# Order of the four pooled-value products of a head pair: by rows first, by heads second

## The chip, the cores and the metric

The kernel runs on one NeuronCore of one Trainium2 chip. The metric is the device time of one execution in microseconds, the median of several runs. TensorE appears in the profile as two engines: PE (matmuls) and PEld (loads of the stationary operand). DVE is VectorE, ACT ScalarE, POOL GpSimd, SP the engine that issues the DMAs.

## The reference

Three layers follow each other. The first is attention over 4 x 8 heads, 576 positions and 64 channels a head, and it is a sum of two parts: a local one (a band of keys around each query) and a pooled one, which the change touches:

```python
q_d = q.reshape(B, H, Sd, factor, D).mean(axis=3)      # factor 4, Sd = 144
k_d = k.reshape(B, H, Sd, factor, D).mean(axis=3)
v_d = v.reshape(B, H, Sd, factor, D).mean(axis=3)
out_d = sm_attn(q_d, k_d, v_d)                         # softmax(q_d k_d^T) v_d
out_up = np.repeat(out_d, factor, axis=2)
...
return (out_up + out_local).astype(np.float32)
```

The second layer is a gated feed-forward (512 to 1024 channels, a convolution of three taps, a sigmoid gate, 1024 back to 512). The third mixes positions with a product of rank 32 and ends with a feed-forward of 512 to 2048 to 512 channels with a ReLU, added to its input.

## The kernel before

The 32 heads are worked on as 16 pairs; the two heads of a pair lie on the partitions 0 to 63 and 64 to 127. All work of all layers is issued in one order written out by hand, the string `SEQ`: each word is a function with its arguments, such as `V.6.0` for the local value products of pair 6 or `Vd.6` for its pooled ones. Each engine runs its part of that list strictly in the order of the list, and waits where data are missing. Attention pairs, the second layer's products (lines 834 and 888) and the decoding of weights are interleaved there up to about 235 us; the third layer follows.

For a pair the pooled part goes so: scores (line 525), their maximum (530), the exponential (537), the division (542), the transposition by TensorE (575 and 576), the copy of the transposed weights to `PTd` (595 to 598), and then `pv_pooled` (from line 611). The 144 pooled keys do not fit on 128 partitions, so they are split into 112 and 32. The values of the first 112 keys lie in `vd`. The last 32 keys of four pairs share one tile `ve`, each pair on its own 32 partitions (`rest(p)`), and `PTd` is split in the same manner. So each head needs two products that add up in PSUM: one that contracts over 112 rows, and one over 32 rows. Each product has 64 stationary columns (a head's channels) and 144 moving columns (the queries). Head 0 writes to the partitions 0 to 63 of the tile `O`, head 1 to 64 to 127, in the same PSUM bank. Data are float32, and the trace shows each product as two weight loads and two matmuls, so a pair's four products are eight of each.

Just before them in `SEQ`, as a rule, stands `pv_local` (line 608): 24 products with 64 rows and 64 stationary columns each. They use the two row halves and the two column halves of the array in turn. Behind the pooled products `copy_od` (`xd`, lines 625 and 627) and `add_x` (line 636) take the sum out of `O`. In the earlier pairs the words `f.n` add filler matmuls (`beat`, line 390) that write to a spare part of the tile used last; where that is `O`, its readers wait for them as well.

The buffers `vd`, `ve` and `PTd` are used again by later pairs, whose pooled sums of values (`vsum`, line 558) and copies wait for the last product that reads the buffer.

Of the kernel before, what the change touches and what calls it, by code (L numbers as in the profile page):

```python
# [276 lines left out]
def mixer_kernel(ctx, tc, consts, qk, vw_, vr_, vz_, w1, w2, cw_, u_, v_, out, outT):  # L277
    nc = tc.nc
# [5 lines left out]
    D = P // 2  # L284
# [9 lines left out]
    SD, NM = S // 4, 112  # L294
# [272 lines left out]
    def rest(p):  # L567
        return slice(32 * (p % 4), 32 * (p % 4) + 32)
# [42 lines left out]
    def pv_pooled(p):  # L611
        e = st[p]
        pt = e["PTd"].rearrange("p c (j r) -> p c j r", j=3)
        for h in range(2):
            o = e["O"][D * h:D * h + D, 0, 288:288 + SD].rearrange("p (j r) -> p j r", j=3)
            to, cols = slice(48 * h, 48 * h + 48), slice(D * h, D * h + D)
            nc.tensor.matmul(o, e["vd"][:, cols], pt[:NM, 0, :, to], start=True, stop=False)  # L617
            nc.tensor.matmul(o, e["ve"][rest(p), cols], pt[rest(p), 1, :, to], start=False, stop=True)  # L618

    def copy_od(p, eng):  # L620
        e = st[p]
# [585 lines left out]
    def flush_t(r, blk, c):  # L1207
# [10 lines left out]
        "Sd": scores_d, "Md": maxima_d, "Ed": exps_d, "nd": lambda p: norm_d(p, GP), "ndv": lambda p: norm_d(p, DV),  # L1218
        "vs": vsum, "vsv": lambda p, i: vsum(p, i, DV), "T": trans, "Td": trans_d, "c": lambda p: copy_T(p, "ACT"), "cv": lambda p: copy_T(p, "DVE"),
        "cd": lambda p: copy_Td(p, A), "cdv": lambda p: copy_Td(p, V), "V": pv_local, "Vd": pv_pooled,  # L1220
        "xd": lambda p: copy_od(p, "ACT"), "xdv": lambda p: copy_od(p, "DVE"), "x": add_x,
        "wl": w_load, "wd": lambda *k: w_dec(DV, *k), "wp": lambda *k: w_dec(GP, *k), "wh": w_hi, "wo": lambda *k: w_lo(GP, *k), "wO": lambda *k: w_lo(DV, *k),
# [96 lines left out]
```

## Time and profile before

| | |
|---|---|
| runs | 714.07, 714.94, 718.48 us; median 714.94 us |
| the profiled execution's own time | 717.92 us |
| its span, first to last instruction | 716.1 us |
| mean granted TensorE clock | 0.989 of 2.4 GHz |
| busy time of PE, PEld, DVE, ACT, POOL | 701.1, 636.6, 543.5, 433.2, 340.7 us |
| instructions in the span | 15851 |

The busy times come from one profiled execution, whose time is 3.0 us above the median of the runs. Busy time of PE counts a matmul from its issue to its modelled end, so neighbouring matmuls overlap and a drained array can still count as busy; idle time of the array at a change between products is seen better on PEld. A granted clock of 1.00 is 2.4 GHz, one of 0.50 is 1.2 GHz.

### The profile page before, as it was taken

The numbers are of one execution on the slowest core, as the hardware profiler recorded it, in microseconds if no ns is written. First come the engines' busy times: TensorE is split into PE (matmuls) and PEld (weight loads), VectorE is DVE, ScalarE is ACT, GpSimd is POOL, SyncE is SP. The second block draws the span as 40 slices with busy tenths as digits, with TensorE's granted clock in tenths as the row PEclk, the third lists the DMA queues.
The fourth block names the chain that finished last, engine by engine and source line by source line (L and its number), as shares of the span: only waits on it lengthen the run. The fifth ranks groups of instructions, "written<-read, shape, count | busy, mean of one in ns | idle before, by whom it ended". The sixth has DMA issues, their size and how long they took to land.

```text
span 716.1 us, 15851 instructions
## 1 busy us (share of the span) xinstructions
PE 701.1 (98%) x5937; PEld 636.6 (89%) x5937; DVE 543.5 (76%) x963; ACT 433.2 (60%) x1005; POOL 340.7 (48%) x353
## 2 busy tenths in 40 slices
PE   6999999999999999999999999999999999999997
PEld 4878788888888888898999988899999999999997
DVE  4878998878876877789886666577756797667777
ACT  4778888676576776888755555555434465443431
POOL 2246465135233553558465646134734463554543
PEclk9979999999999999999999999999999999999999
DMA  8777543534443340224889989889887768687765
GB/s 292 223 248 261 172 138 143 189 126 153 156 127 127 116 133 31 88 89 141 274 284 305 312 299 318 297 274 313 286 277 224 242 195 271 219 278 246 252 205 180
DMA packets 75388, 152.22 MB, mean 213 GB/s; under 512 B 8176, under 2 KB 16624, under 8 KB 75312
## 3 DMA queue, kind: packets, MB, share of 16 engines
q1 hardware_dynamic: 75312, 151.22, 63.2%
q8 instruction: 47, 0.77, 0.5%
q14 instruction: 29, 0.24, 0.1%
HBM read 111.34 MB, written 39.85 MB: 211 GB/s over the span
## 4 chain that ended last, share of the span: by engine, by line
PE 89%; DMA 3%; DVE 2%; issue 2%; POOL 2%; ACT 1%; SPq 1%; DVEq 0%; POOLq 0%; ACTq 0%
PE g L1045 24%; PE acc L888 14%; PE g L834 13%; PE acc L1077 9%; PE xa L1198 8%; PE ya L1198 4%; PE za L1198 2%; PE O L608 2%; PE O L617 1%; PE S L459 1%; PE Sd L525 1%; PE O L618 1%; DMA wb<-t 1%; PE h L912 1%; POOL w L721 1%
## 5 line engine op out<-in xcount | busy, mean ns | idle before, releaser
L1045 PE MATMUL g<-bt,as 128*128 128x384 f32 x1008 | 197.0, 338 | 0.5 <-DMA as<-s 0.5
L1045 PEld LDWEIGHTS g<-bt,as 128*128 128x128 f32 x1008 | 178.6, 188 | 5.3 <-issue 1.0
L834 PE MATMUL g<-xhl,w 128*128 128x386 f32 (+1 forms) x576 | 119.0, 346 | 0.8 <-DVE ghl L880 0.8
L888 PE MATMUL acc<-w,ghl 128*128 128x512 f32 x432 | 114.1, 397 | 0.4 <-DVE ghl L880 0.4
L834 PEld LDWEIGHTS g<-xhl,w 128*128 128x128 f32 x576 | 101.9, 190 | 6.8 <-issue 1.4
L1184 POOL TENSOR_TENSOR rt<-fr,rt 128x384 fp32r<-128x384 f32 x64 | 65.6, 1038 | 62.4 <-ACT rt L1180 56.0
L888 PEld LDWEIGHTS acc<-w,ghl 128*128 128x128 f32 x432 | 79.2, 188 | 15.0 <-issue 1.0
L1205 DVE TENSOR_TENSOR uT<-uT,xa 128x384 f32<-128x384 f32 x128 | 69.1, 551 | 30.0 <-PE xa L1198 29.3
L880 POOL TENSOR_TENSOR ghl<-ct,ghl 128x384 fp32r<-128x384 f32 x40 | 42.7, 1068 | 87.1 <-ACT ghl L877 72.8
L1198 PE MATMUL xa<-rt,wb 128*128 128x384 f32 x384 | 82.4, 337 | 0.1
L1184 POOL TENSOR_TENSOR rt<-tp,rt 128x384 fp32r<-128x384 f32 x48 | 50.5, 1063 | 53.0 <-ACT rt L1180 34.9
L1077 PE MATMUL acc<-w,a 128*128 128x512 f32 x288 | 73.7, 394 | 0.0
L1050 ACT ACTIVATE tp<-g 128x384 f32<-128x384 f32 x72 | 35.2, 488 | 63.5 <-PE g L1045 62.0
L861 DVE SCALAR_TENSOR_TENSOR g<-h,cw,g 128x384 f32<-128x384 f32 x96 | 59.3, 618 | 14.0 <-ACT g L856 12.7
L1198 PEld LDWEIGHTS xa<-rt,wb 128*128 128x128 f32 x384 | 67.8, 188 | 1.0 <-DVE uT L1205 0.8
L1054 DVE TENSOR_TENSOR tp<-g,tp 128x384 f32<-128x384 f32 x72 | 40.0, 555 | 33.5 <-PE g L1045 31.5
L1077 PEld LDWEIGHTS acc<-w,a 128*128 128x128 f32 x288 | 53.2, 188 | 8.7
L1180 ACT ACTIVATE rt<-fr 128x384 fp32r<-128x384 f32 x64 | 32.6, 520 | 25.6 <-PE za L1198 9.2
L1198 PE MATMUL ya<-rt,wb 128*128 128x384 f32 x192 | 42.5, 337 | 1.8 <-DMA wb<-t 1.8
L1205 DVE TENSOR_TENSOR uT<-uT,ya 128x384 f32<-128x384 f32 x64 | 34.6, 549 | 9.6 <-PE ya L1198 9.6
L1107 POOL TENSOR_TENSOR l<-s,l 128x256 fp32r<-128x256 f32 x28 | 22.7, 815 | 34.3 <-ACT l L1103 34.3
L721 POOL TENSOR_TENSOR w<-wval,w 128x512 fp32r<-128x512 f32 x17 | 22.8, 1348 | 28.7 <-ACT w L718 22.8
(182 smaller groups left out, 1303.7 us busy)
## 6 DMA issues: line engine op xcount, KB each, us to landing
as<-s SPq DMA_DIRECT2D x112, 256.0 KB, 4.2
wb<-t SPq DMA_DIRECT2D x112, 256.0 KB, 4.2
s<-as SPq DMA_DIRECT2D x56, 256.0 KB, 3.2
raw<-in_w_dram SPq DMA_DIRECT2D x26, 512.0 KB, 5.1
zraw<-in_w_dram SPq DMA_DIRECT2D x22, 512.0 KB, 4.3
qk<-in_qk_dram SPq DMA_DIRECT2D x16, 576.0 KB, 5.3
t<-l SPq DMA_DIRECT2D x28, 256.0 KB, 2.9
vw<-in_vw_dram SPq DMA_DIRECT2D x16, 384.0 KB, 4.3
```

Source lines behind the costliest of these rows:

```text
L834: nc.tensor.matmul(gp[n][:, :wd], w[:, a, cc], xhl[g, cc][:, b, :wd], start=cc == 0 and i == 0, stop=cc == NCC - 1 and i == 2)
L861: nc.vector.scalar_tensor_tensor(out=o, in0=inner(g, hts[n], k), scalar=cw[:, k * NF + f:k * NF + f + 1], in1=o, op0=ALU.mult, op1=ALU.add)
L880: eng.tensor_tensor(ghl[n][:, 1], cts.pop(n), ghl[n][:, 0].bitcast(F32), op=ALU.subtract)
L888: nc.tensor.matmul(acc[g][c], t[:, a, c * P:(c + 1) * P], w[:, b], start=f == 0 and i == 0, stop=f == NF - 1 and i == 2)
L1045: nc.tensor.matmul(o, w[:, a, k], Bs[r, j, k][:, b, :TB], start=j in (0, 1, 3) and n == 0, stop=n == 3 * HC - 1, skip_group_check=True)
L1050: nc.scalar.activation(out=t[:, :TB], in_=bank[q, 0][:, :TB], func=AF.Copy)
L1054: nc.vector.tensor_tensor(t, bank[q, 1][:, :TB], t, op=ALU.add)
L1077: nc.tensor.matmul(acc2[g][c], t[:, a, c * P:(c + 1) * P], w[:, b], start=f == 0 and n < 2 and i == 0, stop=f == NFP - 1 and n >= 2 and i ...
L1180: nc.scalar.activation(out=t[:, 0], in_=f_src(q, j), func=AF.Copy)
L1184: eng.tensor_tensor(t[:, 1], f_src(q, j), t[:, 0].bitcast(F32), op=ALU.subtract)
L1198: nc.tensor.matmul(o, w[:, a, m * P:m * P + P], t[:, b], start=new and i == 0, stop=i == 2, skip_group_check=True)
L1205: nc.vector.tensor_tensor(u, u, src, op=ALU.add)
```

## The change

The loops over heads and over the two parts of the keys change places. Before, head 0 had its 112-row product and its 32-row product, and then head 1 had the same two. After, the two 112-row products come first, head 0 then head 1, and the two 32-row products follow, head 0 then head 1. Operands, shapes, targets, and the flags that start and end a sum of each head stay as they were. `SEQ` is the same.

```diff
-        for h in range(2):
-            o = e["O"][D * h:D * h + D, 0, 288:288 + SD].rearrange("p (j r) -> p j r", j=3)
-            to, cols = slice(48 * h, 48 * h + 48), slice(D * h, D * h + D)
-            nc.tensor.matmul(o, e["vd"][:, cols], pt[:NM, 0, :, to], start=True, stop=False)
-            nc.tensor.matmul(o, e["ve"][rest(p), cols], pt[rest(p), 1, :, to], start=False, stop=True)
+        parts = ((e["vd"], pt[:NM, 0]), (e["ve"][rest(p)], pt[rest(p), 1]))
+        for c, (v, w) in enumerate(parts):
+            for h in range(2):
+                nc.tensor.matmul(e["O"][D * h:D * h + D, 0, 288:288 + SD].rearrange("p (j r) -> p j r", j=3),
+                                 v[:, D * h:D * h + D], w[:, :, 48 * h:48 * h + 48], start=c == 0, stop=c == 1)
```

## Rows read from the trace of the kernel before

**Rows 1.** The page: busy time, share of the span, instructions of each engine.

```profile
PE 701.1 (98%) x5937; PEld 636.6 (89%) x5937; DVE 543.5 (76%) x963; ACT 433.2 (60%) x1005; POOL 340.7 (48%) x353
```

**Rows 2.** The page: the chain that ended last, by engine and by line.

```profile
PE 89%; DMA 3%; DVE 2%; issue 2%; POOL 2%; ACT 1%; SPq 1%; DVEq 0%; POOLq 0%; ACTq 0%
PE g L1045 24%; PE acc L888 14%; PE g L834 13%; PE acc L1077 9%; PE xa L1198 8%; PE ya L1198 4%; PE za L1198 2%; PE O L608 2%; PE O L617 1%; PE S L459 1%; PE Sd L525 1%; PE O L618 1%; DMA wb<-t 1%; PE h L912 1%; POOL w L721 1%
```

**Rows 3.** Windows by stage: length, busy time (instructions) of each engine, clock, DMA.

```profile
0.00:87.00 87.00, 78.05 (x1419) 63.60 (x1419) 67.06 (x109) 61.48 (x162) 36.21 (x47) 0.92 0.71 241
87.00:137.00 50.00, 49.85 (x735) 43.18 (x739) 46.04 (x77) 42.05 (x106) 24.44 (x24) 1.00 0.47 158
137.00:240.00 103.00, 103.00 (x1271) 87.03 (x1264) 80.27 (x145) 67.94 (x166) 35.68 (x37) 1.00 0.42 139
240.00:716.00 476.00, 470.19 (x2526) 442.81 (x2524) 350.11 (x635) 261.72 (x573) 244.38 (x246) 1.00 0.69 229
```

**Rows 4.** Timeline of one pair: start, length, engine, line, rows*columns, count, idle before.

```profile
136.79 0.92 PE L608 MATMUL O<-PT,vw 64*64 64x48 f32 x48
137.64 0.19 PEld L617 LDWEIGHTS O<-PTd,ve 112*64 112x64 f32 x2
137.64 0.46 PE L617 MATMUL O<-PTd,ve 112*64 112x144 f32 x2
...
138.03 0.19 PEld L618 LDWEIGHTS O<-PTd,ve 32*64 32x64 f32 x2 [0.20 <-issue]
...
138.41 0.19 PEld L617 LDWEIGHTS O<-PTd,ve 112*64 112x64 f32 x2 [0.20 <-issue]
...
138.80 0.19 PEld L618 LDWEIGHTS O<-PTd,ve 32*64 32x64 f32 x2 [0.20 <-issue]
...
139.18 0.48 PEld L834 LDWEIGHTS g<-xhl,w 128*128 128x128 f32 x3 [0.20 <-issue]
```

**Rows 5.** Line 617 from 87 to 240 us: idle time before it.

```profile
  issue: 2.0, 10
```

**Rows 6.** Line 618 from 87 to 240 us: its matmuls, idle time before it.

```profile
L618 PE MATMUL O<-PTd,ve x40: 281/306/332, 93.4 to 233.0; 32*64 32x144 f32 x40
...
  issue: 4.0, 20
```

**Rows 7.** Timeline of the weight loads of one pair's transpositions.

```profile
142.83 0.11 PEld L576 LDWEIGHTS Td<-front,Pd 96*64 96x64 f32 x1
142.91 0.14 PEld L575 LDWEIGHTS Td<-front,Pd 96*128 96x128 f32 x1
...
143.07 0.54 PEld L888 LDWEIGHTS acc<-w,ghl 128*128 128x128 f32 x3
```

**Rows 8.** The chain in order of time: start, length, what.

```profile
44.58 0.67 PE O L617 x2
45.25 0.67 PE O L618 x2
...
63.84 3.28 issue
...
93.04 0.39 PE O L617 x2
...
148.53 0.74 PE Sd L525 x6
...
231.76 0.39 PE O L617 x2
```

**Rows 9.** DVE's timeline: the first reader of the pooled sum that waited long.

```profile
34.11 0.31 DVE L627 TENSOR_SCALAR xd<-O 128x144 f32<-128x144 f32 x1 [1.14 <-PE O L390]
```

**Rows 10.** Short windows around the stretch at a lower clock (columns as in Rows 3).

```profile
39.00:40.00 1.00, 0.09 (x1) 0.09 (x2) 1.00 (x2) 0.54 (x3) 0.97 (x2) 1.00 1.00 394
...
42.00:47.00 5.00, 5.00 (x63) 3.36 (x61) 4.62 (x4) 1.95 (x5) 2.73 (x4) 0.50 0.86 285
47.00:52.00 5.00, 5.00 (x111) 4.57 (x110) 2.08 (x4) 4.68 (x10) 2.07 (x2) 0.50 0.61 218
```

## The prediction

> **What bounds the kernel now.** I read first the busy times [rows 1] and the chain [rows 2]. TensorE is busy 98% of the span and carries 89% of the chain; the next engine, DVE, is busy 76%. So a microsecond taken out of TensorE's own time should come out of the kernel, unless the stage in which it lies is not TensorE's. The pooled products, lines 617 and 618, hold 2% of the chain together.
>
> Then I cut the span into stages [rows 3]. From 87 us to the end PE is without idle time, but for some 6 us late in the third layer. Up to 87 us it is idle for 9 of 87 us, and there the chain changes between engines. Of the 16 pairs' pooled products six lie before 87 us and ten behind it: 40 matmuls of line 618 [rows 6], four a pair. The chain runs through the ten: first and last stand in [rows 8].
>
> The third view is the timeline of one pair [rows 4], where the weight loads show the rhythm. The first product starts at 137.64, the next ones at 138.03, 138.41 and 138.80, and other work at 139.18: 1.54 us for four products, 0.385 us each. Of that the two loads take 0.19, and then PEld is idle for 0.20 with nothing named that it waits for. This repeats: 10 times before line 617 and 20 before line 618 behind 87 us, 0.20 each, 6 us in all [rows 5, 6]. Where does this idle time come from? It stands wherever the number of rows changes: 112 to 32, 32 to 112, 32 to 128. The loads of the transpositions alternate between 64 and 128 columns on the same 96 rows and go on to 128 rows, at 0.08 us a step and with no such gap [rows 7]. So I read it as the array running empty before its rows are divided otherwise.
>
> The Trainium skill says this in "TensorEngine Tiling (Array Packing)", Key Properties: changing the tiling mode, not just the tile, drains the engine. It gives no price; the row's 0.20 us does.
>
> **What the change does.** It removes no instruction and adds none. Per pair the rows now go 64, 112, 32, 112, 32, next work: five changes. After it they go 64, 112, 32, next work: three. What remains are two sections, one of 112 rows and one of 32, each with a product of both heads. The cost of a section is that of one product now, 0.385, plus what the second head adds.
>
> What the second head adds no row shows, so I bound it. *Above:* it waits until the first has streamed. The same 144 columns cost 0.74 us for six matmuls in line 525, 0.123 each [rows 8], so two matmuls add 0.25. *Below:* it runs beside the first, on the other 64 columns of the array, and adds only its issue. The nearest row is line 608 [rows 4]: 48 matmuls from 136.79 to 137.64, 0.85 us, 0.018 each. At line 525's rate 48 columns stream in 0.041, and 48 times that is 1.97 us, so 2.3 matmuls run at a time. The two row halves explain two at most; so products on the same rows and different column halves run together too. I take the lower end, two matmuls of 0.018, 0.035 a section, since line 608 is nearer: it too has 64 columns and targets in one bank, and it changes tile without a gap.
>
> So a pair costs 2 x (0.385 + 0.035) = 0.84 in place of 1.54, and saves 0.70 us; by the upper end it costs 1.27 and saves 0.27.
>
> Where does it count? The ten pairs behind 87 us lie on the chain with a busy PE before and after: 10 x 0.70 = 7.0. Two of them lie in 87 to 137, where DVE is busy 46.0 of 50 [rows 3]; its 4.0 of idle time are more than their 1.4, so I count them in full. From 137 to 240 DVE has 23 us of idle time for 5.6.
>
> Of the six before, three stand on the chain, at 24, 29 and 44.6 us, and the others, at 37, 62 and 84, where other engines end last: nothing. The first two speed up what DVE waits for: it sat idle for 1.14 us for fillers that stand in O behind the second pair's products [rows 9]. I count 1.1 for the two, not 1.4. The third runs at half the clock, 0.67 a product [rows 8], and saves 1.2; but behind it the chain passes to ACT and POOL, and has a 3.28 us hole at 63.84 that names no engine [rows 8]. I count zero there; the ends for all six are 0 and 4.7.
>
> The sum is 7.0 + 1.1 = 8.1 us. In the profiled execution that is 717.92 to 709.8; its time is 3.0 above the median of the runs, which goes from 714.94 to 706.8.
>
> **What else moves.** `SEQ` is the same, so no queue has a new order, SP's and POOL's included. The last of the eight matmuls of a pair is still a 32-row one, so the readers `xd` and the writer of the next `ve` are released 0.70 sooner, and the next `vd` and `PTd` not later. The first product waits for the same copy and the same `vd`. The first product that needs `ve` started 0.385 us after the first of all and will start at 0.42, so a late `ve` has a little more cover than now. The third layer starts 7 to 8 us sooner as a whole; its loads are asked for as its own buffers come free, so I expect its few waits to move along.
>
> **The rivals.**
>
> *Serial heads.* The second head's matmuls wait for the first's. Then a pair saves 0.27, ten pairs 2.7, and 0.4 before 87 us: 3.1 us, 711.8. For it: nothing in the trace shows two matmuls with more than 64 rows side by side. Against it: line 608's 2.3 at a time.
>
> "TensorE: Matmul & The Clock Gate", Part 3, The mechanism, in the Trainium skill speaks for this rival: a load overlaps matmuls in flight only when its row group differs, and matmuls start and end in strict order. By that the two heads, on the same rows, would not overlap. The trace speaks against strict order: two matmuls of each of line 608's products, one behind the other on one tile, would need at least 24 x (0.041 + 0.018) = 1.4 us, and it took 0.85.
>
> *It doesn't do what it says.* If the array drains whenever the tile changes, the change of heads costs 0.20 as the change of rows did, and nothing moves: 714.9. Against it: line 608 changes tile with every product and has no gap.
>
> *Slower.* The engine may take the two heads' matmuls in turn, as the rows of line 608 suggest it does, but drain at each turn with 112 or 32 rows. A section of four matmuls then has four drains in place of two now, so a pair has eight and not four: 4 x 0.20 more, and with 11 pairs that count 9 us, 724. It decides from the third drain in a section on. Against it is the same gapless row.
>
> *The clock.* It fell to 0.50, 1.2 GHz, from 42 to 52 us, after a microsecond with PE busy 0.09 [rows 10]; at full clock that work would take 5 us less. Earlier pairs that end sooner shift the idle stretches before it. If the stretch goes away, the gain is 8.1 + 5, 702; if another like it comes, 712. The profile can't say which.
>
> **Chances.** Parallel heads 0.80, serial 0.12, no effect 0.04, slower 0.04; the clock (0.05 to each side) lies inside these. Within the first case the early pairs give 0 to 4.7 in place of 1.1, DVE may take back 1.4, and the second head may add nothing (0.07 more a pair): 702.5 to 709.3. The range takes in the serial case: 702.5 to 712. One per cent is 7.1 us, about what a measurement of this kernel can tell from no change; 706.8 is 0.9 beyond that, so of the parallel case about two thirds count as faster: 0.55 faster, 0.41 the same, 0.04 slower.
>
> **What would show it.** In the timeline of a pair, two sections of about 0.42 us in place of four of 0.385, one gap of 0.20 before line 618's loads and one before the next work, none between the heads. The idle times before lines 617 and 618 fall from 30 gaps to 10. If sections last 0.63, the heads are serial. The window from 137 to 240 should end 5 to 6 us sooner relative to its start. If the sections shrink and the span doesn't, the gain is lost in waits of PE for DVE or POOL, before 137 us above all; the prediction is wrong too if the clock has other stretches at 0.50.

## The result and the profile after

The changed kernel takes 707.27 us (median of four runs, 704.76 to 707.85), the one before 715.46 (714.07 to 718.48). The ratio is 0.9873 with a 95% interval of 0.9833 to 0.9913: 1.3% faster. The forecast was 706.8, worked out from the three runs on record then, with a median of 714.94.

The profiled execution of after is its fastest, 704.76 us with a span of 703.0; that of before was one of its slowest. So the two traces lie 13.2 us apart where the medians lie 8.2 apart, and positions in them must be compared with that in mind. The lengths inside a pair behind 87 us, all at the full clock, are not touched by it.

The page of after, busy times and the two lines of the chain; they answer to [rows 1, 2]:

```profile
PE 688.1 (98%) x5937; PEld 629.9 (90%) x5937; DVE 541.7 (77%) x963; ACT 432.3 (61%) x1005; POOL 338.5 (48%) x353
...
PE 88%; DVE 3%; DMA 3%; issue 2%; POOL 2%; ACT 1%; SPq 1%; DVEq 0%; POOLq 0%; ACTq 0%
PE g L1045 24%; PE acc L888 14%; PE g L834 13%; PE acc L1077 9%; PE xa L1198 9%; PE ya L1198 4%; PE za L1198 2%; PE S L459 1%; PE O L608 1%; PE Sd L525 1%; DMA wb<-t 1%; PE O L617 1%; PE h L912 1%; DMA vr<-in_vz_dram 1%; POOL w L721 1%
```

As many instructions as before, and TensorE still carries the chain; its busy time fell by 13.0 us, that of DVE by 1.8. All four products of a pair now stand on line 617, and with 1% they are what lines 617 and 618 were with 2%.

The timeline of after around the pair of [rows 4]:

```profile
131.54 0.20 PEld L617 LDWEIGHTS O<-PTd,ve 112*64 112x64 f32 x4
131.54 0.86 PE L617 MATMUL O<-PTd,ve 112*64 112x144 f32 x8
...
131.93 0.19 PEld L617 LDWEIGHTS O<-PTd,ve 32*64 32x64 f32 x4 [0.20 <-issue]
...
132.32 0.30 PEld L834 LDWEIGHTS g<-xhl,w 128*128 128x128 f32 x2 [0.20 <-issue]
```

Two sections of 0.39 in place of four: 0.78 us a pair, not 1.54. Four loads now take the 0.20 that two took, so the second head costs about 0.01 a section. Line 617 from 82 to 230 us, the ten later pairs; the idle time answers to [rows 5, 6]:

```profile
L617 PE MATMUL O<-PTd,ve x48: 281/309/337, 88.1 to 220.8; 32*64 32x144 f32 x40, 112*64 112x144 f32 x8
...
  issue: 2.0, 10
```

The 30 gaps of before are 10. The first matmul with 32 rows of these ten pairs starts at 88.1 and the last at 220.8; in [rows 6] these were 93.4 and 233.0. So in these two traces the six early pairs' stage ends 5.3 us sooner and all sixteen pairs' 12.2. Much of the 5.3 is the clock's (last section). From there to the end the distance hardly grows, to 13.1 between the spans. The windows by stage, which answer to [rows 3]:

```profile
0.00:82.00 82.00, 71.89 (x1420) 60.72 (x1421) 67.49 (x110) 61.57 (x163) 36.15 (x47) 0.94 0.76 256
82.00:131.00 49.00, 48.89 (x743) 42.43 (x747) 45.89 (x76) 41.91 (x106) 23.76 (x25) 1.00 0.50 161
131.00:228.00 97.00, 97.00 (x1268) 84.22 (x1260) 81.07 (x145) 68.14 (x168) 35.53 (x37) 1.00 0.45 147
228.00:703.00 475.00, 470.31 (x2524) 442.55 (x2523) 347.25 (x635) 260.66 (x573) 243.04 (x246) 1.00 0.68 230
```

PE stays without idle time from 131 to 228, and the third layer takes 475 us against 476: nothing in it took the gain back. In 82 to 131, DVE is busy 45.89 of 49.

### The profile page after: what moved, and what is told of

Read it like the earlier page. It is cut to its first block, busy times and chain, and to the rows that moved or that the text cites. A ratio compares the mean times of both kernels' runs of the same rounds, so it can differ in the third digit from the quotient of the medians.

```text
span 703.0 us, 15851 instructions
## 1 busy us (share of the span) xinstructions
PE 688.1 (98%) x5937; PEld 629.9 (90%) x5937; DVE 541.7 (77%) x963; ACT 432.3 (61%) x1005; POOL 338.5 (48%) x353
## 4 chain that ended last, share of the span: by engine, by line
PE 88%; DVE 3%; DMA 3%; issue 2%; POOL 2%; ACT 1%; SPq 1%; DVEq 0%; POOLq 0%; ACTq 0%
PE g L1045 24%; PE acc L888 14%; PE g L834 13%; PE acc L1077 9%; PE xa L1198 9%; PE ya L1198 4%; PE za L1198 2%; PE S L459 1%; PE O L608 1%; PE Sd L525 1%; DMA wb<-t 1%; PE O L617 1%; PE h L912 1%; DMA vr<-in_vz_dram 1%; POOL w L721 1%
```

## The experiments

Two questions: where in the kernel does the gain arise, and what in a pair gives it, the changes of the array's division that fall away or the heads that run side by side? The theory says both: a change costs some 0.15 us beside the stream, two of them fall away (0.3), and in two sections the second head's stream of 0.24 is hidden (0.5), together 0.76. All kernels differ from the changed one in `pv_pooled` alone, but for one. Gains below are worked out from the ratio to the kernel before in the same job and its median there (715.65 or 715.69 us).

**Late pairs and early pairs.** The new order in some pairs only; the early kernel has `p < 6`.

```diff
...
+        steps = [(c, h) for c in range(2) for h in range(2)] if p >= 6 else [(c, h) for h in range(2) for c in range(2)]
+        for c, h in steps:
+            v, w = parts[c]
...
```

> Only the pairs 6 to 15, whose pooled products lie behind 87 us, have the new order. Theory: each of them saves 0.76 us (1.546 us of the old order less 0.786 of the new), TensorE has no idle time there, so all of it counts: 10 x 0.76 = 7.6 us, some 707.5. The forecast's sum said 7.0. Rival: other engines, DVE above all, take part of it back, and the kernel gains 5 us or less.

> Only the pairs 0 to 5, before 87 us, have the new order. The forecast counted 1.1 us here: about 714. Rival: all six save 0.76 and the other engines of this stretch wait for TensorE after all, 4.6 us: about 710.5. By the second, the ends of this and of the late pairs' kernel add up to more than the whole change gained (8.2 us).

Measured: the late pairs alone 707.83 us, ratio 0.9899 (0.9873 to 0.9925), a gain of 7.2 us (5.4 to 9.1); the early pairs alone 713.03 us, ratio 0.9972 (0.9952 to 0.9992), 2.0 us (0.6 to 3.4). The late pairs carry what the theory says, 10 x 0.76 = 7.6; the rival's 5 us or less lies outside the interval (though the traces show 0.7 us of it taken back, below). The early six carry less than the 4.6 that they save on TensorE. Together the two gain 9.2, as much as the whole change by its ratio (0.9873 of 715.46: 9.1 us).

**Parts with 32 rows first.** The two sections exchanged.

```diff
-        parts = ((e["vd"], pt[:NM, 0]), (e["ve"][rest(p)], pt[rest(p), 1]))
+        parts = ((e["ve"][rest(p)], pt[rest(p), 1]), (e["vd"], pt[:NM, 0]))
```

> The new order with its two sections exchanged: both heads with 32 rows, then both with 112 rows. Theory: only a change of the number of row strips in use drains the array, and 112 rows and the 128 of the next work are the same to it. Then the last gap of 0.20 goes: the weight loads of the next work follow after about 0.6 us in place of 0.786, the matmuls come some 0.15 earlier, 16 x 0.15 = 2.4 us faster than the changed kernel, 705. Rival: the array drains whenever another operand shape follows, 112 then 128 too: three gaps as in the changed kernel, 707.

Measured: 706.50 us, ratio 0.9876 (0.9852 to 0.9901), not to be told from the change itself. Its weight loads:

```profile
132.38 0.19 PEld L617 LDWEIGHTS O<-PTd,ve 32*64 32x64 f32 x4
132.78 0.20 PEld L617 LDWEIGHTS O<-PTd,ve 112*64 112x64 f32 x4 [0.20 <-issue]
133.17 0.30 PEld L834 LDWEIGHTS g<-xhl,w 128*128 128x128 f32 x2 [0.20 <-issue]
```

The theory (a strip is 32 rows, so that 112 and 128 rows both use four) falls in one point: from 112 rows x 64 columns to 128 x 128 there is the same gap of 0.20, and a pair lasts 0.79. In [rows 7] the transpositions go on from 96 rows to 128 without a gap, so it is not the rows alone.

**Heads with 32 rows first.** The old loops, head outside, with the 32-row product ahead of the 112-row one in each head:

```diff
-        parts = ((e["vd"], pt[:NM, 0]), (e["ve"][rest(p)], pt[rest(p), 1]))
-        for c, (v, w) in enumerate(parts):
-            for h in range(2):
+        parts = ((e["ve"][rest(p)], pt[rest(p), 1]), (e["vd"], pt[:NM, 0]))
+        for h in range(2):
+            for c, (v, w) in enumerate(parts):
```

> The old order by heads, with 32 rows ahead of 112 in each head. No head runs beside the other; the number of row strips changes four times a pair in place of five. Theory of the drain: one gap of 0.20 less, 0.15 us a pair, 16 x 0.15 = 2.4 us: about 712.5. Rival: the gain of the change came from the heads running side by side alone and the gaps are something else: no difference, 715.

Measured: 714.06 us, ratio 0.9987 (0.9970 to 1.0004). Its loads from the first to the next work:

```profile
133.88 0.19 PEld L617 LDWEIGHTS O<-PTd,ve 32*64 32x64 f32 x2
134.27 0.19 PEld L617 LDWEIGHTS O<-PTd,ve 112*64 112x64 f32 x2 [0.20 <-issue]
...
135.43 0.30 PEld L834 LDWEIGHTS g<-xhl,w 128*128 128x128 f32 x2 [0.20 <-issue]
```

1.55 us, four gaps, as in the kernel before. The kernel's time is as the rival said, but the trace tells another reason: the gap that should have gone is there. So this run doesn't separate the two halves of the gain. The next ones do.

**One column half.** The new order, but head 1's sum goes to the partitions 0 to 63 as well:

```diff
-                nc.tensor.matmul(e["O"][D * h:D * h + D, 0, 288:288 + SD].rearrange("p (j r) -> p j r", j=3),
+                nc.tensor.matmul(e["O"][:D, h, 288:288 + SD].rearrange("p (j r) -> p j r", j=3),
...
+        for h in range(2):
+            to, src = t[D * h:D * h + D], e["O"][:D, h, 288:288 + SD]
...
```

> The new order, but head 1 writes to the partitions 0 to 63 too, in the other bank of O, so that both heads use the same column half of the array; the sum is taken out by two copies of 64 partitions. Where fillers follow they write over head 1's sum. The number of changes of rows is that of the changed kernel. Theory (heads run side by side because they use different column halves): here they run one behind the other, a section costs 0.386 + 0.24 and a pair 1.25 to 1.27 us in place of 0.786; some 711.5. Rival (the gain is the two gaps less): a pair stays at 0.79, some 707.

Its loads in one pair:

```profile
136.00 0.44 PEld L617 LDWEIGHTS O<-PTd,ve 112*64 112x64 f32 x4
136.64 0.43 PEld L617 LDWEIGHTS O<-PTd,ve 32*64 32x64 f32 x4 [0.20 <-issue]
137.27 0.30 PEld L835 LDWEIGHTS g<-xhl,w 128*128 128x128 f32 x2 [0.20 <-issue]
```

A pair lasts 1.27 us: the heads run one behind the other, with two changes less than before. That gives both halves: from 1.55 to 1.27 the two changes, 0.28; from 1.27 to 0.79 the second heads' streams, 0.48. The kernel's own time, 714.05 us with a ratio of 0.9990 (0.9968 to 1.0013), is a gain of 0.7 us (at most 2.3), less than 0.28 x 16 = 4.5 and than the 3.4 that the whole change's rate of 12 us for each us in a pair would give. Half or more of what is missing goes with the clock: seven of this kernel's ten runs have a mean granted clock of 0.990 or less, but five of the nineteen of the kernel before in the same job. Compared at like clocks the gain is 2.1 us above 0.990 (713.07, three runs, against 715.14, fourteen) and 2.8 at 0.989 and 0.990 (714.15 against 716.98, five runs each), near the 3.4. These are few runs, and why this kernel met the lower clock more often isn't known. It also copies each sum in two instructions of 0.30 us in place of one; what that costs was not tried.

**All four products with 112 rows, by heads.** The old order, but no change inside a pair:

```diff
-        parts = ((e["vd"], pt[:NM, 0]), (e["ve"][rest(p)], pt[rest(p), 1]))
-        for c, (v, w) in enumerate(parts):
-            for h in range(2):
+        parts = ((e["vd"], pt[:NM, 0]), (e["vd"], pt[:NM, 0]))
+        for h in range(2):
+            for c, (v, w) in enumerate(parts):
```

> The old order by heads, but the products with 32 rows are replaced by a second product over the first 112 keys, so the last 32 keys are left out of the pooled sum. No change of rows inside a pair any more. Theory: the order by heads doesn't keep the heads apart, the change of rows between their products does; so the heads run side by side here as well, 0.386 + 0.24 + 0.01 = 0.64 us a pair, some 705.5. Rival: the matmuls are taken strictly in order, 4 x 0.24 + 0.15 = 1.1 us a pair, some 711.

Measured: 705.03 us, ratio 0.9870 (0.9845 to 0.9895). Its loads:

```profile
131.56 0.45 PEld L617 LDWEIGHTS O<-PTd,ve 112*64 112x64 f32 x8
132.21 0.30 PEld L834 LDWEIGHTS g<-xhl,w 128*128 128x128 f32 x2 [0.20 <-issue]
```

0.65 us for four products of 0.24 us each, listed by heads: they run two at a time. So the old order by heads didn't keep the heads apart. The change of rows between a head's two products did: what stands behind it in the list can't start before what stands ahead has drained. It also means that TensorE doesn't keep the list's order strictly, as the section on the kernel says of every engine: the pair's matmuls start two by two, 0.01 us apart, and with every start in the list's order seven streams of 0.12 and the 0.15 would make 1.0 even where the heads overlap. Whether the engine itself takes them out of order, or they reach it in another order than the list's, the trace doesn't record.

**Queries split.** More changes, with the heads side by side:

```diff
...
+        for a in range(2):
+            for c, (v, w) in enumerate(parts):
+                for h in range(2):
+                    nc.tensor.matmul(e["O"][D * h:D * h + D, 0, 288:288 + SD].rearrange("p (j r) -> p j r", j=3)[:, :, 24 * a:24 * a + 24],
+                                     v[:, D * h:D * h + D], w[:, :, 48 * h + 24 * a:48 * h + 24 * a + 24], start=c == 0, stop=c == 1)
```

> The new order with the moving columns cut in two: both sections for 24 of the 48 queries of each block, then both for the other 24. A pair has eight products of 72 columns, four sections, five changes of rows as the old kernel, and the heads side by side as in the new one. Theory: a section costs its stream, 0.12 in place of 0.24, its first load and a fixed price of the change of about 0.15: 0.28, a pair 1.12 us, some 711. Rival: the changes cost nothing of their own and only the streams that are hidden count: 0.79 a pair, 707. Second rival: every section costs the same 0.39 whatever it streams: 1.57 a pair, 715.5.

Measured: 710.56 us, ratio 0.9938 (0.9919 to 0.9956), a gain of 4.4 us. Its loads in one pair (the four sections are merged into one row):

```profile
135.01 1.01 PEld L618 LDWEIGHTS O<-PTd,ve 112*64 112x64 f32 x16
136.10 0.30 PEld L835 LDWEIGHTS g<-xhl,w 128*128 128x128 f32 x2
```

1.09 us a pair where the theory said 1.12 and the rivals 0.79 and 1.57. A section of half the stream costs 0.27, one of the whole stream 0.39: the stream of 0.12 and a fixed 0.15. The idle time of the loads isn't that price: it is 0.20 behind a stream of 0.24, and here, ahead of the next work, 0.08 (135.01 + 1.01 to 136.10) behind one of 0.12, while the change costs the same.

No version clearly beats the changed kernel. The all-112 one is 2 us ahead by its median, with intervals that overlap, and leaves keys out; a correct form would need the other pairs' rows of `PTd` at zero, and was not tried.

## Why the prediction was right

*The bound.* TensorE's own time came out of the kernel's time nearly one for one from 87 us on: ten pairs save 7.6 on TensorE, and the kernel with only these in the new order gains 7.2 (5.4 to 9.1). From 137 us on nothing was lost: the stretch from the first load of the pair in [rows 4] to the start of the last pair's last product, eight pairs, lasted 233.0 - 137.64 = 95.4 us before and 220.8 - 131.54 = 89.3 after: 6.1 less, eight times 0.76, where the prediction's last part asked for 5 to 6. That the whole comes so near, 8.1 forecast and 8.2 between the medians, is partly luck: the gain by the ratio is 9.1 with an interval of 6.2 to 11.9, and the 0.7 us taken back before 137 (below) hides the 0.6 by which the ten pairs save more than forecast.

*A pair.* 0.84 us were forecast, 0.79 measured. The term that was off is what the second head adds, 0.035 a section by line 608's pace; it is 0.01, since TensorE's two column halves also take their loads side by side. The choice of the lower bound was right, and the run with one column half shows that the upper one, 0.25 a section, is what happens where the heads can't run together (0.24).

*What a change costs.* The prediction took the 0.20 us of idle loads for the price of a change. The price is 0.15, a section's 0.39 less its stream of 0.24; the sum didn't use the 0.20, but whole sections; only the slower rival's 724 did.

*Where the gap comes from.* The prediction read the gap as a change of the number of rows. The reading is too narrow: it drew on the transpositions [rows 7], where 64 and 128 stationary columns alternate without a gap, but from the pooled products' 112 x 64 to 128 x 128 there is one. The sum wasn't hit, because in the new order both sections end in a change of rows in any case. What marks off the two kinds of 64 columns, the transpositions' and the products', these runs don't show.

*The early pairs.* 1.1 us were counted for six pairs, and 2.0 (0.6 to 3.4) measured. The first two moved what [rows 9] names, DVE's reader of the second pair's sum:

```profile
32.32 0.31 DVE L627 TENSOR_SCALAR xd<-O 128x144 f32<-128x144 f32 x1 [0.39 <-PE O L390]
```

34.11 became 32.32, and the wait 0.39 instead of 1.14. It is the order that does this: the wait is 1.14 again in the kernel with the late pairs alone, whose early pairs have the old order, and 0.18 in the one with the early pairs alone. From the first pair's first product to this read it took 9.86 us before (24.25 to 34.11) and 8.34 after (23.98 to 32.32), so both pairs' 0.76 arrived there in full, more than the wait of 1.14 that the forecast took for the limit. By the third pair's first product 0.8 of that is left: 12.97 us from the first pair's before (24.25 to 37.22), 12.14 after (23.98 to 36.12). By how much each of the other four counts can't be told from these runs: the clock moves this stage by more (below).

*DVE between 87 and 137.* Counted in full, with the wait as a risk. In the traces the ten late pairs' positions gain 6.9 us (12.2 less 5.3), 0.7 short of 7.6, and the eight from 137 on lose nothing, so it is the first two that fall short. There PEld has two waits in after that before has not, 0.5 us of line 452 and the shorter, 0.2, of line 834's two:

```profile
PEld g L834 <- DVE ghl L880: 1.7, 2, 1.5
...
PEld S L452 <- PE acc L888: 0.5, 1, 0.5
```

Line 834's longer wait, 1.5, ends at 81.89, ahead of these pairs, and before has it too, with 1.1 at 87.15. The same two waits stand in the kernel with the late pairs alone, and neither does in the one with the early pairs alone, so they come with the new order. So a little came back there, as the prediction allowed; but DVE is named for 0.2 of it, and what freed line 452, the scores of a later pair, isn't settled.

*The clock.* The prediction gave other stretches at 0.50 as a sign of being wrong. They came, as the last section shows, and the sum held all the same. The sign was badly chosen: the kernel before differs in its stretches from run to run too, with mean clocks of 0.989 to 0.998.

*The rivals.* Serial heads are refuted for this order and shown for the kernel with one column half. The Trainium skill's "TensorE: Matmul & The Clock Gate", Part 3, The mechanism, says that a load overlaps matmuls in flight only where its row group differs, and that matmuls start and end in strict order. By both the all-112 kernel's pair, in the order of the list, would have needed 1.1 us; it took 0.65, so the trace disagrees for products on the same rows and different column halves. The other rule of the Trainium skill that was named, "TensorEngine Tiling (Array Packing)", Key Properties, that a change of mode drains and a change of tile doesn't, agrees: 0.15 us a change, and 0.01 for a change of head inside a section. No effect and the slower rival are out: there is no gap between the heads.

## What to carry to other kernels

Small products that differ in how they divide TensorE's array should be sorted by that division first: a change cost 0.15 us here, and worse, it keeps apart products that would run side by side in different halves of the array, 0.24 us each time. Look on the weight loads' row of a timeline for idle times that name no releaser; the busy share of PE hides them, because a draining array counts as busy. Take the price from the distance of the products' starts less their stream, not from the gap. What it is worth is its count on the chain: sixteen pairs of 0.76 us here, of which the ten in TensorE's own stage came through nearly whole.

## What the runs showed of the hardware

The stretch at half the clock comes and goes without a change in the code. In the kernel with the new order in the late pairs only, everything up to 87 us is as in the kernel before, and yet there is no such stretch where [rows 10] has one (columns as in [rows 3]):

```profile
42.00:47.00 5.00, 4.96 (x163) 3.87 (x161) 5.00 (x5) 3.16 (x8) 2.44 (x3) 1.00 0.89 282
47.00:52.00 5.00, 4.30 (x44) 3.92 (x30) 4.18 (x8) 4.98 (x11) 2.08 (x2) 1.00 0.87 292
```

Its first pooled product behind 87 us starts at 89.53, against 92.97 in the kernel before, by its timeline:

```profile
89.53 0.20 PEld L618 LDWEIGHTS O<-PTd,vd 112*64 112x64 f32 x4
```

That is 3.4 us before any changed instruction. At the first product of the first pair it is 0.4 (24.25 against 23.89), at that of the third still 0.4 (37.22 against 36.86), and at that of the fifth 3.4 (62.46 against 59.04). Between the third and the fifth lies the stretch of [rows 10], and no other in which the clocks differ. So its 10 us cost some 3 us in these two traces, and not the 5 that the prediction took: at the full clock PE does the work sooner and then sits idle for part of what it saves, 0.70 of the 5.00 us from 47 to 52.

Both have an earlier stretch at the half clock, first before, then the late pairs' kernel:

```profile
18.00:21.00 3.00, 3.00 (x107) 2.75 (x106) 2.96 (x4) 2.25 (x6) 1.09 (x2) 0.50 0.82 247
...
17.00:22.00 5.00, 5.00 (x115) 4.75 (x115) 4.02 (x7) 3.52 (x9) 0.25 (x1) 0.50 0.88 277
```

In after the half clock lies from 15 to 22 us too, ahead of the first pairs, and again for a short stretch behind 39 us:

```profile
15.00:18.00 3.00, 2.29 (x60) 2.10 (x62) 2.59 (x4) 2.46 (x6) 2.45 (x3) 0.55 0.94 343
18.00:22.00 4.00, 4.00 (x79) 3.92 (x73) 3.23 (x7) 2.72 (x7) 0.00 (x0) 0.50 0.93 295
...
39.00:42.00 3.00, 3.00 (x29) 2.79 (x33) 2.94 (x4) 2.08 (x6) 2.92 (x4) 0.53 1.01 371
```

So part of the 13.2 us between the two profiled executions is the clock's, and the medians of several runs are what the change is judged by. Over the 42 runs of the kernel before in the experiments' two jobs, the ten with a mean clock of 0.990 or less have a median of 717.3 us and the nine with 0.997 or more one of 713.9: 3.4 us apart in the same program. So it pays to compare the clocks too before a difference of that size between two kernels is believed. The clock isn't all of it: among the four runs of after the slowest, 707.85 us, had the highest mean clock, 0.998, and the fastest 0.992. What else differs between runs of one kernel stays open.
